# An mLSTM cell and a gated feed-forward block: the state's increments by products of 32 and of 8 weight columns instead of 40

## The chip, the cores and the metric

The kernel runs on one core of one Trainium2 chip. The metric is the device time in microseconds (us). The core has five engines that work side by side: TensorE (PE in the profile, its weight loads PEld) multiplies matrices, VectorE (DVE), ScalarE (ACT) and GpSimd (POOL) work element by element, and SyncE (SP) issues most of the transfers (DMAs). Matmul results land in PSUM, a memory of 128 partitions; all other tiles are in SBUF.

## The reference

Two blocks, one behind the other. The first is a recurrent cell over 768 steps, for 4 batches (B) and 8 heads (H) of 40 dimensions (D). Each head has a state `C` of 40 x 40 and a normalizer `n` of 40:

```python
for t in range(S):
    m_new = np.maximum(f_gate[:, :, t] + m, i_gate[:, :, t])
    f_stab = np.exp(f_gate[:, :, t] + m - m_new)
    i_stab = np.exp(i_gate[:, :, t] - m_new)
    C = f_stab * C + i_stab * outer(vt, kt)          # per batch and head
    n = f_stab * n + i_stab * kt
    y[:, :, t] = sigmoid(o_gate[:, :, t]) * (C @ qt) / max(abs(n @ qt), 1)
```

(shown with the subscripts of batch and head left out). The second block takes the 3072 x 320 rows that come out: `h = x @ w_in` (320 x 2048), `g = h * cos(h)`, `out = g @ w_out` (2048 x 320).

## The kernel before

**Cells.** The sequence is cut into six chunks of 128 steps. A cell is one chunk of one batch, all eight heads; cell n is chunk n // 4 of batch n % 4, so there are 24. Within a cell the recurrence is done as products over the 128 steps. The state of each batch (`st[b]`) is carried from chunk to chunk: after a cell it is faded and an increment is added, the sum over 128 steps of weighted keys times values. This increment is what the change is about. It is needed for all chunks but the last, so in cells 0 to 19.

**The increment.** `weigh_k` (line 408) makes the weighted keys `kw` on GpSimd, 128 steps x 8 heads x 64, of which 40 columns are used. `seam(n)` (line 586) multiplies on TensorE: for each of four pairs p of heads and each j of a pair, the 128 x 40 keys are the weights that are loaded and 48 value columns (`DV`: 40 of values and 8 of ones, for the normalizer) move past them. The 40 x 48 result lands in the PSUM tile `pu`, on partitions 64 j to 64 j + 40, in column block p. So two products, j = 0 and j = 1, stand side by side in `pu`, and four pairs behind each other. A product of float32 numbers is done in two passes, and has two weight loads (LDWEIGHTS) and two matmuls (MATMUL) in the profile: 20 cells x 8 products are 320 records of each.

**Who stands before and behind.** `seam` is called by `first_cells` for the cells 0 to 3, by `first_period` for cell 4 and by `both_parts` for the others. In cells 0 to 3 it first turns the cell's output with four products (`px`, lines 592 and 594; those of 594 load 64 weight columns) and then makes the increment; behind it come the products of the next cell (`ph`, line 491) or warming matmuls. From cell 4 on there is no `px`: the increment follows directly on `values(n)` (line 483), whose products `vt` (lines 501 to 510) load 32 weight columns, or 16, move 128, and land four side by side on partitions 32 a:

```python
nc.tensor.matmul(vt[32 * a:32 * a + 32, i], vs(n)[:, h, 0:32], E[:, h], start=True, stop=False)
```

Behind it come the products of the second block's next pair of hidden tiles (`pup`, lines 644 and 650).

**Who reads `pu`.** `state(n)` (line 619) adds it to `st[b]`, in four pieces: on ScalarE (line 625) for cells 0 to 3, on VectorE (line 627) for the others. It reads partitions 64 j to 64 j + 40, as before. The loads of k and v of later cells (`load_two`, line 330, on SyncE's queue) write into buffers that `weigh_k` and the increment's products have read.

**The second block** is woven between the cells, in chunks of 512 rows (four batches): class `Up` (line 632) makes pairs of hidden tiles `pup`, ScalarE and VectorE make `g` from them (`near`, `rest`, `sin`, `gate`, lines 657 to 672), and `down` (line 674) or `products` (line 731, tile `acc`) multiply by `w_out`. In the first 130 us or so the weights come in, as pairs of 32-bit words that lines 144 to 162 turn into float32.

**Order.** The order of the instructions on every engine is written out by hand (`first_cells`, `first_period`, `both_parts` under a manual schedule); each engine works through its own queue in that order, and semaphores are put in where a tile is handed over. SyncE's queue issues transfers in the order written.

Of the kernel before, what the change touches and what calls it, by code (L numbers as in the profile page):

```python
# [29 lines left out]
def kernel(  # L30
# [20 lines left out]
    nc = tc.nc  # L51

    B, H, S, D = q.shape
# [231 lines left out]
    sig, xT, xL, Es, kws, qkT, pss, heads_of, raw_o, Gs, early = {}, {}, {}, {}, {}, {}, {}, {}, {}, {}, {}  # L285
# [10 lines left out]
    def vs(n):  # L296
        return vs2[n // 2 % 2][:, n % 2]
# [121 lines left out]
    def psum(n):  # L419

        return (ps_o, "o") if n < B and n % 2 == 1 else (ps_a, "a")
# [164 lines left out]
    def seam(n):  # L586

        pool, tag = psum(n)
        if n < B:
            px = pool.tile([128, NK + 1, C], FP, name="px", tag=tag)  # L590
            for i in range(NK):
                nc.tensor.transpose(px[:, i], ys[n][:, ts(i, 128)], ident)
            for e in range(2):
                nc.tensor.matmul(px[64 * e:64 * e + 64, NK], ys[n][:, KL:DM], ident, start=True, stop=True)
            pxs[n] = px
        if n < N - B:
            pu = pool.tile([128, HP, DV], FP, name="pu", tag=tag)
            for p in range(HP):
                for j in range(2):
                    h = 2 * p + j  # L600
                    nc.tensor.matmul(pu[64 * j:64 * j + D, p], kws[n][:, h, 0:D], vs(n)[:, h], start=True, stop=True)  # L601
            pus[n] = pu

    def low_out(n):
# [229 lines left out]
    def first_cells():  # L834
# [53 lines left out]
        turn_out(2, False)  # L888
        warm(2)
        seam(0)  # L890
        weigh(1)
        seam_out(0)
# [10 lines left out]
        turn(3)  # L903
        sigmoid(0, slice(2, 4))
        seam(1)
        load_two(B, "Kv")
        outs.append((0, weights_out(0)))
# [10 lines left out]
        scores(3)  # L918
        warm(1)
        seam(2)  # L920
        weigh(3)
        take_apart(*pieces[0])
# [245 lines left out]
```

## Time and profile before

| | |
|---|---|
| time, median of 3 runs | 534.6 us (534.35 to 534.88) |
| profiled execution: its own time | 531.87 us |
| profiled execution: span from first to last instruction | 530.1 us |
| mean granted TensorE clock in it | 0.988 |
| TensorE's weight loads, busy | 346.9 us |
| VectorE busy | 406.9 us |
| ScalarE busy | 286.6 us |
| GpSimd busy | 247.9 us |
| moved by DMA | 57.81 MB |

The profile is of one execution, and its durations are of that one. A row of a group tells the line of the code, the engine, the operation, the tile written and those read, the shapes (128*40 128x48 is 128 rows by 40 weight columns, with 48 moving columns on 128 partitions) and how many there were. Matmuls overlap each other, and their ends are modelled; so differences of starts say more than durations, and the chain of waits, which goes back from the last instruction to what released each step, says which engine's time counts. "issue" stands for time in which an engine waited for nothing that the profile shows.

The group of the changed line, by the view of one line (duration in ns: least, median, most; first and last start):

```profile
L601 PEld LDWEIGHTS pu<-vs,kw x320: 112/117/184, 22.9 to 361.6; 128*40 128x40 f32 x160
L601 PE MATMUL pu<-vs,kw x320: 206/206/303, 23.0 to 361.7; 128*40 128x48 f32 x160
```

### The profile page before, as it was taken

To read this page: it belongs to the slowest core of one execution; us is meant where nothing else is said; L and a number is where in the kernel's file an instruction comes from. 1 tells how busy PE (TensorE), PEld (TensorE's weight loads), DVE (VectorE), ACT (ScalarE), POOL (GpSimd) and SP (SyncE) were. 2 spreads that over 40 slices of the span, in tenths; PEclk is the share of its full clock that TensorE was granted. 3 is DMA by queue.
4 is the path that set the end of the run, shared out by engine and by line. 5 is a ranking of instruction groups with operands and counts; after the bars stand their busy time and mean duration, and the time that the engine had idled before them with its cause. 6 is when DMAs were issued, how large, how long until landed. Compare 5 with 4: busy or idle time off the path is not lost.

```text
span 530.1 us, 10427 instructions
## 1 busy us (share of the span) xinstructions
PE 512.8 (97%) x3848; PEld 346.9 (65%) x3848; DVE 406.9 (77%) x828; ACT 286.6 (54%) x546; POOL 247.9 (47%) x409
## 2 busy tenths in 40 slices
PE   7999779999999999999999999999999999999996
PEld 3875354556657666676677677677667676666765
DVE  4896798997778878888778888868898878664636
ACT  2896797857556537744547635537735531312221
POOL 7536454673775684554454554453433333121211
PEclk9999879999999999999999999999999999999999
DMA  9999999999339259149159149159110000000001
GB/s 139 227 183 213 231 195 231 246 238 208 48 118 196 56 109 181 41 120 170 56 116 157 42 113 176 49 116 160 47 56 6 1 6 6 26 25 1 1 0 50
DMA packets 97762, 57.81 MB, mean 109 GB/s; under 512 B 62048, under 2 KB 89792, under 8 KB 97712
## 3 DMA queue, kind: packets, MB, share of 16 engines
q1 hardware_dynamic: 96240, 55.64, 51.1%
q0 software_dynamic: 1424, 1.49, 1.4%
q8 instruction: 30, 0.49, 0.4%
q14 instruction: 20, 0.16, 0.1%
q10 hardware_dynamic: 48, 0.02, 0.0%
HBM read 51.71 MB, written 4.11 MB: 105 GB/s over the span
## 4 chain that ended last, share of the span: by engine, by line
PE 81%; DVE 7%; DMA 6%; POOL 1%; issue 1%; SPq 1%; ACT 1%; DVEq 0%; POOLq 0%
PE pup L650 26%; PE acc L760 25%; PE pup L644 8%; PE ps L475 4%; PE po L682 3%; PE late L760 3%; DMA bits<-in_moe_w_in_dram 3%; PE vt L510 2%; PE vt L501 2%; PE pu L601 2%; DMA o<-in_o_gate_dram 1%; PE pw L832 1%; DVE t L456 1%; PE ph L491 1%; DMA bits<-in_moe_w_out_dram 1%
## 5 line engine op out<-in xcount | busy, mean ns | idle before, releaser
L650 PE MATMUL pup<-xT,w_in_sb 128*128 128x512 f32 x384 | 176.7, 603 | 3.1 <-DVE g L670 2.9
L658 ACT ACTIVATE n<-pup 128x512 int32<-128x512 f32 x96 | 54.0, 595 | 193.6 <-PE pup L644 141.6
L650 PEld LDWEIGHTS pup<-xT,w_in_sb 128*128 128x128 f32 x384 | 70.4, 191 | 90.3 <-issue 88.0
L661 DVE SCALAR_TENSOR_TENSOR n<-pup,n 128x512 f32<-128x512 f32 x96 | 63.0, 687 | 82.3 <-ACT n L658 80.9
L724 POOL TENSOR_TENSOR D<-g 128x128 f32<-128x128 f32 x40 | 19.7, 492 | 145.6 <-DVE g L670 145.6
L666 ACT ACTIVATE n<-n 128x512 f32<-128x512 f32 x96 | 59.3, 631 | 16.1 <-DVE n L661 16.1
L670 DVE SCALAR_TENSOR_TENSOR g<-pup,n 128x512 f32<-128x512 f32 x96 | 61.9, 684 | 2.2 <-ACT n L666 1.4
L760 PE MATMUL acc<-w_out_sb,g 128*128 128x160 f32 x320 | 58.6, 304 | 0.0
L760 PE MATMUL acc<-T,g 128*128 128x160 f32 x320 | 58.0, 301 | 0.1
L644 PE MATMUL pup<-xL,w_in_l 64*128 64x512 f32 x192 | 55.2, 650 | 0.9 <-POOL w_in_l L162 0.9
L607 POOL DMA_DIRECT2D xL<-xT x40 | 22.5, 563 | 65.1 <-DVE xT L538 61.6
L760 PEld LDWEIGHTS acc<-w_out_sb,g 128*128 128x128 f32 x320 | 47.8, 190 | 5.6 <-issue 4.2
L760 PEld LDWEIGHTS acc<-T,g 128*128 128x128 f32 x320 | 48.1, 190 | 3.7 <-issue 3.0
L406 ACT ACTIVATE E<-E,tab 128x128 f32<-128x128 f32 x160 | 49.0, 389 | 0.2
L682 PE MATMUL po<-w_out_sb,g 128*128 128x320 f32 x128 | 36.2, 436 | 0.0
L760 PE MATMUL acc<-T,S 128*128 128x160 f32 x160 | 35.0, 300 | 0.0
L475 PEld LDWEIGHTS ps<-t,t 40*128 40x128 f32 (+1 forms) x384 | 24.2, 187 | 12.6 <-DVE t L456 7.5
L682 PEld LDWEIGHTS po<-w_out_sb,g 128*128 128x128 f32 x128 | 24.0, 190 | 11.9 <-issue 1.9
L481 DVE TENSOR_TENSOR E<-ps,E 128x512 f32<-128x512 f32 x48 | 30.7, 680 | 1.4 <-PE ps L475 1.3
L644 PEld LDWEIGHTS pup<-xL,w_in_l 64*128 64x128 f32 x192 | 14.8, 187 | 24.0 <-issue 19.6
L760 PE MATMUL acc<-w_out_sb,S 128*128 128x160 f32 x160 | 28.8, 299 | 0.0
L962 ACT ACT_TABLE_LOAD x22 | 28.2, 1283 | 0.4
(178 smaller groups left out, 878.0 us busy)
## 6 DMA issues: line engine op xcount, KB each, us to landing
E<-M_d SPq DMA_DIRECT2D x22, 512.0 KB, 4.3
qr<-in_q_dram SPq DMA_DIRECT2D x36, 160.0 KB, 3.1
kr<-in_k_dram SPq DMA_DIRECT2D x36, 160.0 KB, 5.4
G<-G_d SPq DMA_DIRECT2D x20, 256.0 KB, 5.2
bits<-in_moe_w_out_dram SPq DMA_DIRECT2D x8, 640.0 KB, 5.8
bits<-in_moe_w_in_dram SPq DMA_DIRECT2D x16, 256.0 KB, 7.6
out_dram<-o_sb SPq DMA_DIRECT2D x24, 160.0 KB, 1.9
ks<-in_k_dram SPq DMA_DIRECT2D x10, 320.0 KB, 7.5
```

The lines of the kernel that those rows point to most:

```text
L406: nc.scalar.activation(out=Es[n][:, h], in_=Es[n][:, h], func=AF.Exp, scale=-1.0, bias=tab[:, c, 0, g:g + 1])
L475: nc.tensor.matmul(ps[j][:, p], kT[r, p], qT[r, p], start=True, stop=True)
L481: nc.vector.tensor_tensor(out=w, in0=pss[n][j], in1=w, op=OP.mult)
L644: nc.tensor.matmul(pu, w_in_l[r, f2], xL[c][r].rearrange("p b t -> p (b t)"), start=ahead, stop=not ahead)
L650: nc.tensor.matmul(pu.rearrange("p (b t) -> p b t", b=B), w_in_sb[:, i, ts(2 * f2 + e, 128)], xT[c][:, i:NK * B:NK], start=(i == 0 and not ...
L658: nc.scalar.activation(out=self.n[e], in_=self.pu[e], func=AF.Copy, bias=0.25)
L661: nc.vector.scalar_tensor_tensor(out=self.n[e].bitcast(FP), in0=self.pu[e], scalar=0.25, in1=self.n[e], op0=OP.add, op1=OP.subtract)
L666: nc.scalar.activation(out=r, in_=r, func=AF.Sin, scale=TWO_PI_DOWN)
L670: nc.vector.scalar_tensor_tensor(out=g, in0=self.pu[e], scalar=TWO_PI, in1=self.n[e].bitcast(FP), op0=OP.mult, op1=OP.mult)
L682: nc.tensor.matmul(po[c][b], gs[c, f][:, ts(b, C)], w_out_sb[:, f], start=(f == 0), stop=(f == NF - 1))
L760: nc.tensor.matmul(a, lhs, rhs, start=start, stop=stop)
L962: nc.scalar.activation(out=spot, in_=spot, func=AF.Sin)
```

## The change

In `seam`, each product of 40 weight columns is made as two: one of the columns 0 to 32, whose result goes to the partitions 64 j to 64 j + 32, and one of the columns 32 to 40, whose result goes to the partitions 64 j + 32 to 64 j + 40. Both move the same 48 value columns. The results lie where they lay before, and nothing else is changed.

```diff
             for p in range(HP):
                 for j in range(2):
                     h = 2 * p + j
-                    nc.tensor.matmul(pu[64 * j:64 * j + D, p], kws[n][:, h, 0:D], vs(n)[:, h], start=True, stop=True)
+                    for lo, hi in ((0, 32), (32, D)):
+                        nc.tensor.matmul(pu[64 * j + lo:64 * j + hi, p], kws[n][:, h, lo:hi], vs(n)[:, h], start=True, stop=True)
             pus[n] = pu
```

The line numbers behind line 600 are one higher in the changed kernel.

## The prediction

> **What bounds the kernel now.** First the page's busy line and its slices, then the chain of waits (what ended last, in order of time), then the timeline around one cell's increments, then the waits of TensorE and of the DMA queue.
>
> ```profile
> PE 512.8 (97%) x3848; PEld 346.9 (65%) x3848; DVE 406.9 (77%) x828; ACT 286.6 (54%) x546; POOL 247.9 (47%) x409
> ...
> DMA  9999999999339259149159149159110000000001
> ```
>
> TensorE is busy 97% of the span. The DMA slices are 13.25 us each (530.1 / 40): ten nines mean that the DMA engines are full for the first 132 us. In that stretch the chain of waits mixes engines (it holds weight transfers at 42.95, 82.57 and 108.77 us). From 116.34 us to 381 us it names TensorE alone; the waits of TensorE between 140 and 375 us have not one entry. So a nanosecond off TensorE in that stretch is a nanosecond off the end, and before it one has to ask.
>
> The changed products are the eight of line 601 in each cell, two matmul records each (320 in 20 cells). The chain of waits at cell 8, one piece to a row (start us, us, what):
>
> ```profile
> 144.04 0.22 PE vt L504 x8
> 144.26 0.22 PE vt L507 x8
> 144.48 0.22 PE vt L510 x8
> 144.70 0.47 PE pu L601 x16
> 145.17 1.06 PE pup L644 x4
> ```
>
> And the same products in cell 1, behind other neighbours:
>
> ```profile
> 27.54 0.22 PE px L592 x2
> 27.76 0.37 PE px L594 x4
> 28.13 0.34 PE pu L601 x16
> 28.47 1.91 PE ph L491 x16
> ```
>
> Sixteen records of one kind cost 0.47 us in cell 8 and 0.34 us in cell 1. What differs is what stands before them. Shapes tell it: vt's products load 32 or 16 weight columns, pu's 40, px L594's 64, px L592's 128. The built program marks the part of the array for each: 32 columns wide for vt, 64 for pu and for L594, 128 for L592. Behind the same width there is no surcharge (L504 to L507 to L510, though 16 columns follow 32; L594 to pu). Behind another width there is: pu after vt 0.47 against 0.34, px L594 0.37 for four records where vt takes 0.22 for eight of the same 128 moving columns.
>
> Where the surcharge sits, in the timeline of cell 7 (start us, us, engine, line, shapes, count, idle before):
>
> ```profile
> 123.05 0.40 PE L507 MATMUL vt<-E,vr 128*16 128x128 f32 x8
> ...
> 123.27 0.40 PE L510 MATMUL vt<-qG,st 128*32 128x128 f32 x8
> 123.60 0.41 PEld L601 LDWEIGHTS pu<-vs,kw 128*40 128x40 f32 x16 [0.20 <-issue]
> 123.60 0.54 PE L601 MATMUL pu<-vs,kw 128*40 128x48 f32 x16
> ```
>
> vt's groups begin 0.22 us apart; pu begins 0.33 us after the last. Its first weight load could not be brought forward under vt's products, as every load inside vt is.
>
> **The change part by part.** Each product of 40 weight columns becomes one of 32 and one of 8, on neighbouring parts of the array, marked 32 wide. Nothing moves in any queue, no wait is added and no DMA touched; the order of all other instructions on the five engines is the same. TensorE gets 160 more products, 320 more matmul records and as many weight loads.
>
> (1) *Entry from vt, cells 4 to 19.* vt and pu are now of one width, so the surcharge of 0.47 - 0.34 = 0.13 us goes. Bounds: 0 if the gap had another cause, 0.13 if it goes whole. I take 0.13, by the three same-width borders above.
>
> (2) *The products themselves.* Now two parts of the array work side by side, so 16 records are 8 passes: 0.34 / 8 = 42.5 ns a pass of 48 moving columns. After, four parts side by side, 32 records, again 8 passes. No row shows four parts with 48 columns. From below: 42.5 ns, the present pass, since the same 48 columns go through. From above: the four go two by two, 85 ns. vt is nearest, it has four parts of 32 columns: 8 records are two passes in 0.22 us, 0.11 us for 128 columns, 0.86 ns a column, or 41 ns for 48. So 42.5 ns, and the products cost what they cost. That four can start fast enough is seen in a slice of the timeline 30 ns wide:
>
> ```profile
> 142.96 0.32 PE L501 MATMUL vt<-E,vs 128*32 128x128 f32 x4
> ```
>
> Four records of some 0.30 us each (mean 286 ns) fit into 0.32 us: their starts lie within about 20 ns, 7 ns apart. Four starts of 7 ns are 28 ns, less than a pass; the two added parts put the last start 0.014 us later, which I leave in the rounding.
>
> (3) *Weight loads.* 32 + 8 + 32 + 8 = 80 columns a pass, as 40 + 40 = 80 now; no more to load in the same time, only in more pieces.
>
> (4) *Exit to L644 (or ph L491).* A change of width before, and one after: 0.
>
> (5) *Entry from px L594, cells 0 to 3.* These were of one width with pu and no longer are: the 0.13 us appears there. For cells 0, 1 and 2 pu is on the chain (at 23.18, 28.13, 32.81 us); in cell 3 the chain has left through px to ScalarE. So +0.4 us at most. What can cover it is the DMA: the chain runs into transfers at 42.95 us (6.57 us), 49.54 (7.59) and 57.15 (4.69), at times when all 16 DMA engines are full, so that a request made later only waits less. From 0 to +0.4; I take half, +0.2.
>
> (6) *Cells 4, 5 and 6, before the 116 us mark.* 0.13 us less each on TensorE, of which cells 5 (78.53 us, 0.82 us at a low clock) and 6 (101.94 us) lie on the chain. The queue of loads hangs on these products:
>
> ```profile
> SPq L345 <- PE pup L650: 20.8, 8, 3.4
> ...
> SPq L345 <- PE pu L601: 4.6, 1, 4.6
> ```
>
> (waits of the DMA queue: total us, times, longest). An earlier end lets the load of k and v go earlier, into full DMA engines. From 0 to -0.4; I take -0.2, and (5) and (6) cancel.
>
> (7) *Cells 7 to 19*, from 123.4 us on, 13 cells on the pure TensorE chain: 13 x 0.13 = 1.7 us. Is there room for it on the other engines? In the densest stretch read (220 to 240 us) VectorE is busy 18.05 of 20 us; a cell of about 20 us gets 0.13 us shorter, and 1.95 us are free. Behind pu stands L644, which needs the buffers that gate L670 frees; in cell 8 that gate ended at 142.03 us, 3 us ahead of L644.
>
> Sum: -1.7 + 0.2 - 0.2 = -1.7 us, bounds of (5) and (6) included -2.1 to -1.3. The profiled execution took 531.87 us (span 530.1 and 1.8 around it): 530.2 after. The median of the runs is 534.6, 2.7 above that execution, so I carry the difference over: **532.9 us**.
>
> One rule speaks against (2). The Trainium skill, page "TensorE: Matmul & The Clock Gate", section "Wait — 56ns, not 53.3ns?", says that matmuls start no closer than about 25 ns however few columns they move. By that, 32 records would be an estimated 0.80 us, 0.33 more than now, and 13 cells would cost 4.3 us: 538.9. The trace does not bear it out across parts of the array: pu's 16 records in 0.34 us are 21 ns apart on average, and vt's four start 7 ns apart.
>
> **The rivals.**
>
> *A floor per record (slower).* If the 21 ns per record of today (0.34 / 16) are what issuing a load and a matmul takes, and not the 48 columns, then 32 records take 0.68 us. That is +0.21 us in cells 4 to 19, and +0.34 with the new surcharge of 0.13, so +0.47, in cells 0 to 2. 13 x 0.21 = +2.7; the early cells add 0 to 3 x 0.47 + 3 x 0.21 = 2.0. Middle +3.7: 538.3 us. It decides from 0.47 / 32 = 15 ns a record on. For it: no row sustains more than one record in 21 ns. Against it: the 7 ns starts, and that 42.5 ns a pass is just what 48 columns take at vt's 0.86 ns a column, so that the columns explain the whole pass.
>
> *The gap before pu is a wait, not a width.* The waits of line 601 put 12 of its 16 gaps down to vt L507 and 4 to nothing. If pu really waited for vt's products, the late start (0.33 - 0.22 = 0.11 us) would stay and only the slower first pass be saved, some 0.02: 13 x 0.02 = 0.3 us, 534.3. Against: the gaps are some 0.2 us whichever name they carry, and px L594 has one (0.17) behind L592 with no wait at all.
>
> *The gain is swallowed.* Either the first cells cost their whole 0.4 and the middle ones give nothing, or another engine takes the time back at the borders between chunks, where VectorE is on the chain (381 to 394 us). 1.7 - 0.4 = 1.3, less about half: -0.6, 534.0. For it: 14 us of VectorE on the chain there. Against: that stretch begins with vt L510 on TensorE, so it moves forward with it.
>
> *The change does not do what it says.* Other marks of the array than assumed: the built program has 32-wide ones for all 16 products, so I give it nothing.
>
> **How the numbers follow.** Forecast 0.68 (532.9, own range 532.3 to 533.4: the bounds of (5) and (6), and 0.1 to 0.2 for the medians, whose three runs lie within 0.5). Wait or swallowed together 0.21 (534.0 to 534.6). Floor 0.09 (537.3 to 539.3), 0.02 for anything else slower. This measurement can tell about 0.2%, 1.07 us, from no change: below 533.53 is faster, 0.69 with the edge of the swallowed case; within, 0.20; slower, 0.11. The range 532.1 to 534.7 holds all but the floor and the odd cases.
>
> **What would show it.** Right: in the chain, pu from cell 4 on at about 0.34 us with 32 records, vt's last group to pu 0.22 us, no idle time before its weight load; in cells 0 to 2 about 0.47. TensorE's start-to-start from vt's last group to L644 falls from 0.80 us (123.27 to 124.07) to about 0.67. L644's own 1.06 is unchanged. Wrong: pu near 0.68 (floor), pu still 0.11 us late (a wait), or pu at 0.34 with the span of 116 to 376 us unshortened (swallowed).

## The result, and the profile after

The changed kernel took 531.35 us (median of 10 runs, 530.14 to 532.59) against 534.01 us for the kernel before in the same measurement (10 runs, 532.83 to 534.88). The ratio is 0.9951, with a 95% interval of 0.9937 to 0.9964: 2.7 us faster, between 1.9 and 3.4. The forecast was 1.7 us faster and 532.9 us, in a range of 532.1 to 534.7; the time lies below that range. Three more measurements of the same kernel, told below, give a smaller gain: 2.1 us over all four.

The profiled execution of the changed kernel has a span of 530.2 us (531.94 us in all), that of before 530.1 us. The two single executions are as long as each other, because the stretch before cell 7 happened to take 117.7 us in the one and 116.3 in the other; the change shows in them all the same. The chain of waits at cell 8, one piece to a row (start us, us, what); line 602 is the old line 601, 645 the old 644, 651 the old 650, 671 the old 670:

```profile
145.15 0.22 PE vt L504 x8
145.36 0.22 PE vt L507 x8
145.58 0.22 PE vt L510 x8
145.80 0.34 PE pu L602 x32
146.14 1.06 PE pup L645 x4
```

Twice as many records, and 0.34 us instead of 0.47. The timeline of the same place has pu 0.22 us behind vt's last group, as one vt group stands behind another:

```profile
145.18 0.40 PE L507 MATMUL vt<-E,vr 128*16 128x128 f32 x8
145.40 0.40 PE L510 MATMUL vt<-qG,st 128*32 128x128 f32 x8
145.62 0.52 PE L602 MATMUL pu<-vs,kw 128*32 128x48 f32 x32
146.07 1.13 PE L645 MATMUL pup<-xL,w_in_l 64*128 64x512 f32 x4
```

From vt's last group to L645 it is 0.67 us, where it was 0.80. The view of line 602 has no wait for vt L507 any more; four gaps are left, those of cells 0 to 3:

```profile
L602 PE MATMUL pu<-vs,kw x640: 206/206/230, 22.0 to 361.8; 128*32 128x48 f32 x132, 128*8 128x48 f32 x28
...
  issue: 0.7, 4
```

There the gap that was foreseen has come. In the timeline of weight loads at cell 1, L594 loads 64 columns, and pu's first load starts only after a gap of 0.17 us; in the trace of before there is no gap at this place:

```profile
26.67 0.20 PEld L594 LDWEIGHTS px<-ident,y 128*64 128x64 f32 x4 [0.17 <-DVE E L481]
27.04 0.41 PEld L602 LDWEIGHTS pu<-vs,kw 128*32 128x32 f32 x32 [0.17 <-issue]
```

**Where the saving went.** The start of each TensorE product in the trace of after, less the start of the same product in the trace of before, steps down by 0.130 or 0.131 us at each of the 13 increments from cell 7 to cell 19, 1.70 us together. But it steps up again in five places: at 153.08 us of the old trace (0.13), 176.79 (0.10), about 195 (0.07), 234.71 (0.10) and 314.77 (0.10), 0.50 together. The chain of after at the first of them:

```profile
150.83 3.26 PE acc L761 x24
154.09 0.10 issue
154.19 3.67 PE pup L651 x8
157.86 1.06 PE pup L645 x4
158.92 1.02 PE ps L475 x16
```

`pup` products of this kind, between `acc` and L645, take 3.43 us elsewhere in this chain (at 173.35 us), and `ps` 0.89. What they wait for is in VectorE's timeline:

```profile
151.25 1.29 DVE L662 SCALAR_TENSOR_TENSOR n<-pup,n 128x512 f32<-128x512 f32 x2 [2.15 <-ACT n L659]
152.46 0.86 DVE L628 TENSOR_TENSOR st<-st,pu 40x128 f32<-40x128 f32 x4
153.35 1.29 DVE L671 SCALAR_TENSOR_TENSOR g<-pup,n 128x512 f32<-128x512 f32 x2
```

The first of the two gates of L671 ends at about 154.0 us and frees the buffer into which `pup` is written from 154.19 on. The four additions of the state (L628, 0.86 us) stand ahead of it. At the other four places it is the turning of k (L456), which ends just as `ps` begins:

```profile
176.55 1.07 DVE L456 STREAM_TRANSPOSE t<-kr 128x512 f32<-128x512 f32 x1
...
177.67 0.97 PEld L475 LDWEIGHTS ps<-t,t 40*128 40x128 f32 x16 [0.66 <-DVE t L456]
```

So of 1.70 us on TensorE 1.20 reach the end. That was to be seen before the change, in two views. The old chain has

```profile
153.12 3.64 PE pup L650 x8
...
157.81 0.99 PE ps L475 x16
```

where rows of the same kind are 3.43 (at 172.35 us) and 0.89 (at 176.84): at 153.12 VectorE is late already. At the four turnings the rows of the old chain are 0.89 or 0.94, and there it is the weight loads that show how close VectorE is. In the old trace the first load of `ps` stands like this at one of the four places (176.55) and at one that lost nothing (254.18):

```profile
176.55 0.99 PEld L475 LDWEIGHTS ps<-t,t 40*128 40x128 f32 x16 [0.54 <-DVE t L456]
...
254.18 0.19 PEld L475 LDWEIGHTS ps<-t,t 40*128 40x128 f32 x2 [0.24 <-issue]
```

At the four places the turning of k ended 0.11 to 0.18 us before `ps` began, and 0.6 to 1.4 us before it elsewhere from cell 8 on, but for cell 9, whose `ps` (the row at 157.81) was waiting already. The waits of TensorE's matmuls name none of this, because in the profile the matmul ahead is still running while the load waits; those of its weight loads between 140 and 375 us do (us in total, times, longest):

```profile
PEld ps L475 <- DVE t L456: 3.1, 6, 0.7
```

### The profile page after: what moved, and what is told of

It reads as the page before. It is cut to its first block, busy times and chain, and to the rows that moved or that the text cites. A ratio compares the mean times of both kernels' runs of the same rounds, so it can differ in the third digit from the quotient of the medians.

```text
span 530.2 us, 11067 instructions
## 1 busy us (share of the span) xinstructions
PE 510.7 (96%) x4168; PEld 347.7 (66%) x4168; DVE 405.3 (76%) x828; ACT 286.6 (54%) x546; POOL 247.8 (47%) x409
## 4 chain that ended last, share of the span: by engine, by line
PE 78%; DMA 8%; DVE 4%; ACT 3%; SPq 3%; POOL 2%; issue 1%; DVEq 0%; ACTq 0%; POOLq 0%
PE pup L651 27%; PE acc L761 25%; PE pup L645 8%; PE po L683 4%; PE ps L475 3%; PE late L761 3%; PE vt L510 2%; PE vt L501 2%; DMA bits<-in_moe_w_out_dram 2%; DMA E<-M_d 2%; DMA low<-in_moe_w_in_dram 1%; DMA G<-G_d 1%; DMA bits<-in_moe_w_in_dram 1%; PE pu L602 1%; SPq L328 1%
## 5 line engine op out<-in xcount | busy, mean ns | idle before, releaser
L671 DVE SCALAR_TENSOR_TENSOR g<-pup,n 128x512 f32<-128x512 f32 x96 | 61.9, 684 | 2.3 <-ACT n L667 1.5
L645 PE MATMUL pup<-xL,w_in_l 64*128 64x512 f32 x192 | 54.2, 641 | 1.4 <-POOL w_in_l L162 1.3
L683 PE MATMUL po<-w_out_sb,g 128*128 128x320 f32 x128 | 37.4, 446 | 0.1
L645 PEld LDWEIGHTS pup<-xL,w_in_l 64*128 64x128 f32 x192 | 14.4, 184 | 24.9 <-issue 20.2
```

Of the source, the lines that this page charges most:

```text
L645: nc.tensor.matmul(pu, w_in_l[r, f2], xL[c][r].rearrange("p b t -> p (b t)"), start=ahead, stop=not ahead)
L671: nc.vector.scalar_tensor_tensor(out=g, in0=self.pu[e], scalar=TWO_PI, in1=self.n[e].bitcast(FP), op0=OP.mult, op1=OP.mult)
L683: nc.tensor.matmul(po[c][b], gs[c, f][:, ts(b, C)], w_out_sb[:, f], start=(f == 0), stop=(f == NF - 1))
```

## The experiments

All but the first row are timed in five rounds, beside the kernel before on the same chip. The "late stretch" is the time in one trace from cell 7's first score product to the last instruction. Over seven traces with the old products in it (before and the kernels below) it is 413.66 to 413.85 us, so it repeats to 0.2 us; what comes before it, with the DMA engines full, takes 116.3 to 120.1 us.

| kernel | median us (runs) | before us (runs) | ratio (95%) | late stretch us |
|---|---|---|---|---|
| changed, first measurement | 531.35 (10) | 534.01 (10) | 0.9951 (0.9937 to 0.9964) | 412.48 |
| only_first | 533.46 (12) | 533.66 (35) | 1.0005 (0.9982 to 1.0028) | 413.85 |
| only_mid | 533.28 (12) | 533.66 (35) | 0.9991 (0.9974 to 1.0007) | 413.80 |
| only_late | 532.13 (12) | 533.66 (35) | 0.9965 (0.9946 to 0.9984) | 412.58 |
| all_again | 531.59 (12) | 533.66 (35) | 0.9961 (0.9945 to 0.9978) | 412.57 |
| moving_halves | 536.54 (12) | 533.90 (29) | 1.0049 (1.0033 to 1.0065) | 417.05 |
| only_rest | 531.54 (12) | 533.90 (29) | 0.9962 (0.9945 to 0.9980) | 412.46 |
| vector_ahead | 530.40 (6) | 533.90 (29) | 0.9932 (0.9910 to 0.9954) | 411.71 |
| vector_ahead_old_width | 532.53 (12) | 533.90 (29) | 0.9976 (0.9957 to 0.9995) | 412.97 |
| mid_thrice | 533.19 (12) | 533.39 (24) | 0.9991 (0.9978 to 1.0004) | 413.68 |
| first_thrice | 534.31 (12) | 533.39 (24) | 1.0017 (0.9998 to 1.0036) | 413.79 |
| vector_ahead_narrow | 529.77 (6) | 533.39 (24) | 0.9928 (0.9908 to 0.9948) | 411.16 |
| all_third | 531.36 (8) | 533.39 (24) | 0.9949 (0.9929 to 0.9969) | 412.58 |
| unchanged | 534.29 (12) | 533.43 (35) | 1.0012 (0.9995 to 1.0029) | 413.66 |
| all_fourth | 531.73 (12) | 533.43 (35) | 0.9964 (0.9946 to 0.9983) | 412.44 |
| only_late_again | 531.34 (12) | 533.43 (35) | 0.9966 (0.9949 to 0.9984) | 412.44 |
| only_mid_again | 533.02 (12) | 533.43 (35) | 0.9989 (0.9975 to 1.0002) | 413.78 |

### The change by its cells

Three kernels split the increment in some cells alone, one is the changed kernel again.

```diff
-                    for lo, hi in ((0, 32), (32, D)):
+                    for lo, hi in ((0, 32), (32, D)) if n < B else ((0, D),):             # only_first
+                    for lo, hi in ((0, 32), (32, D)) if B <= n < B + 3 else ((0, D),):    # only_mid
+                    for lo, hi in ((0, 32), (32, D)) if n >= B + 3 else ((0, D),):        # only_late
```

only_first:

> Only cells 0 to 3 are split; their increments follow px of another width, and the entry costs 0.13 us each in the trace in every theory. Theory P (as predicted: three entries on the chain, half hidden by the DMA): +0.2 us, between 0 and +0.4. Theory F (the unexplained 1.5 us of the early stage come from these cells, whose later end shifts what the transfers collide with): -1.0 to -1.5 us. Theory S (any more TensorE records shift the early stage, wherever they stand): about -0.5 us.

only_mid:

> Only cells 4, 5 and 6 are split; each saves 0.13 us on TensorE. Theory P: -0.2 us, between 0 and -0.4. Theory M (the earlier end lets the loads of k and v go earlier, and the early stage gains by more than the time saved on TensorE): -1.0 to -1.5 us. Theory F: 0 to -0.4.

only_late:

> Only cells 7 to 19 are split. By the trace of the change 8 of the 13 savings of 0.13 us come through and 5 turn into new waits for VectorE: -1.1 us (theories F and M). If all of the measured difference comes from here, -2.6 us; if the new waits are an accident of that execution, -1.7 us.

all_again:

> The changed kernel once more on the same chip, as the yardstick: -2.6 us (interval of the first measurement -1.9 to -3.4). If the parts add up, only_first + only_mid + only_late give the same. If it comes out near -1.1 to -1.7, the early stage had given nothing and the first measurement lay high.

The late cells alone give -1.9 us by the ratio (-2.9 to -0.9), and -1.2 in the late stretch (413.75 to 412.58); the five steps back stand in this trace at the same places and of the same size, so they are no accident. The first cells give 0.3 us (-1.0 to +1.5), the middle ones -0.5 (-1.4 to +0.4): the intervals hold the forecast's +0.2 and -0.2, and shut out that either is worth 1.5, though not that the middle ones are worth 1. The parts add to -2.1, which is all_again's own -2.1. So the first measurement gave 0.5 us more than its repeat.

### More records without the narrower width

moving_halves keeps 40 weight columns and moves the 48 value columns in two halves.

```diff
-                    nc.tensor.matmul(pu[64 * j:64 * j + D, p], kws[n][:, h, 0:D], vs(n)[:, h], start=True, stop=True)
+                    for lo, hi in ((0, DV // 2), (DV // 2, DV)):
+                        nc.tensor.matmul(pu[64 * j:64 * j + D, p, lo:hi], kws[n][:, h, 0:D], vs(n)[:, h, lo:hi], start=True, stop=True)
```

> Twice the matmul records at the old width: all 40 weight columns, the 48 value columns moved as 24 and 24. Width theory: the entry of 0.13 us stays, a pass of 24 columns takes 20 to 23 ns, so 32 records take 0.34 to 0.40 us behind the same 0.13: 0 to +0.06 us a cell, 0 to +1.0 us in all. Floor theory (21 ns for each record): 0.68 us and the entry, +0.34 us a cell, +4 to +7 us. If more records alone made the kernel faster, as the change did: -1 us or better.

It is 2.6 us slower, and neither number fits. The timeline at cell 8:

```profile
145.97 0.40 PE L510 MATMUL vt<-qG,st 128*32 128x128 f32 x8
146.31 0.82 PE L602 MATMUL pu<-vs,kw 128*40 128x24 f32 x32
147.06 1.13 PE L645 MATMUL pup<-xL,w_in_l 64*128 64x512 f32 x4
```

The entry is there as in the old kernel (0.34 us after vt's group), since the width is the old one. But the 32 records start over 0.62 us: 16 passes of 38 to 39 ns each, hardly less than the 42.5 ns of 48 columns. The width theory had 20 to 23. What stayed the same is what is loaded, 40 columns, and the likeliest reading is that a pass on one part of the array is no shorter than the loading of its weights; ph of line 491, which loads 128 columns and moves 41, agrees with 1.91 us for 16 records, 119 ns each. A floor of 38 ns for one part of the array, whatever it loads, was not told apart from this. It is no price of a record over the whole array: in the changed kernel 32 records start over 0.32 us, 10 ns each, because four parts of the array share them. So more TensorE records at the old width make the kernel slower, not faster.

### Cells 4 to 19, and VectorE out of the way

only_rest splits in cells 4 to 19 (`n >= B`). vector_ahead takes the five waits away: in the second half of each period, from the second chunk on, the gates come before the state's additions, and q and k are turned before the sums.

```diff
-                if cell:
+                if cell and c == 0:
                     state(n)
                 for e in range(2):
                     up.sin(e)
                     up.gate(e)
+                if cell and c > 0:
+                    state(n)
+                    if n + 1 < N:
+                        turn_blocks(n + 1)
                 if c > 0:
                     sums(c, f2)
...
                 if cell and n + 1 < N:
-                    turn_blocks(n + 1)
+                    if c == 0:
+                        turn_blocks(n + 1)
                     scale_q(n + 1)
```

only_rest:

> Cells 4 to 19 split, cells 0 to 3 as before. The stretch from cell 7's scores to the end loses 1.2 us as in the changed kernel (413.8 to 412.5 us). Theory P (the early entries cost, half hidden): 0.2 us faster than the changed kernel, about -2.4 us against before. Theory F (the first cells' split helps the early stage): only -1.2 to -1.7 us.

vector_ahead:

> The changed kernel, and from the second chunk on VectorE makes the gates before it adds the state's increments, and turns q and k before it makes the sums. If the five savings of 0.13 us were lost in waits for VectorE, these waits go and the stretch from cell 7's scores to the end falls from 412.5 to 412.1 us or below: 0.5 us or more faster than the changed kernel, about -2.6 to -3.5 us against before. If the five waits have another cause, the stretch stays at 412.5 us.

vector_ahead_old_width:

> The same order on VectorE with the old products of 40 columns. The trace of before shows some 0.5 us of waits for VectorE in the stretch from cell 7's scores on (413.8 us). If only those go: 413.3 to 413.8 us, 0 to -0.5 us against before, and the split is then worth its full 13 x 0.13 = 1.7 us between this kernel and vector_ahead. If the new order is worth as much with either width, the split is worth 1.2 us between the two.

only_rest gives -2.0 us by the ratio, with all_again's -2.1; the first four cells' split is neither a help nor a loss that can be seen. vector_ahead is at 530.40 us, its ratio 0.9932. Its chain at the place of the first wait:

```profile
151.54 3.26 PE acc L761 x24
154.80 3.43 PE pup L651 x8
158.23 1.06 PE pup L645 x4
159.29 0.89 PE ps L475 x16
```

3.43 and 0.89: the waits are gone, and with them every step back between cells 8 and 19. The late stretch of this trace is 411.71 us; the execution lost 0.45 us at 137 us, where vector_ahead_narrow, told below, has the same code, loses nothing and comes to 411.16. With the old width the new order gives 412.97 us. Product by product, the starts of vector_ahead_narrow less those of vector_ahead_old_width step down by 0.130 or 0.131 us at each of the 13 increments and nowhere up: the split's 1.70 us come through whole when VectorE is out of the way. This shows the five waits to be the cause of what was missing.

The order by itself is worth 0.8 us of 413.75 with the old width, more than the 0 to 0.5 that were expected. Against the trace of before, 0.3 us of it come where VectorE was late already (from 153 to 196 us), and 0.4 at 394 us: the chain of before runs over VectorE from 381 to 394 us, and that of vector_ahead_old_width stays on TensorE there.

### The early cells, with larger levers

mid_thrice and first_thrice issue each product three times with the same result, on the old width, in cells 4 to 6 or in cells 0 to 3. The expectations take 0.68 us more for a cell; in the traces it is 0.80 (the row of pu in the chain is 1.27 us instead of 0.47 in cell 6, and 1.14 instead of 0.34 in cells 0 to 2), so 2.4 us more in cells 4 to 6, and as much in cells 0 to 2. vector_ahead_narrow is vector_ahead with `px` of 32 columns in cells 0 to 3.

```diff
+                    for _ in range(3 if B <= n < B + 3 else 1):       # mid_thrice; first_thrice: n < B
                         nc.tensor.matmul(pu[64 * j:64 * j + D, p], kws[n][:, h, 0:D], vs(n)[:, h], start=True, stop=True)
...
-                nc.tensor.matmul(px[64 * e:64 * e + 64, NK], ys[n][:, KL:DM], ident, start=True, stop=True)
+                for lo in (0, 32):                                    # vector_ahead_narrow
+                    nc.tensor.matmul(px[64 * e + lo:64 * e + lo + 32, NK], ys[n][:, KL + lo:KL + lo + 32], ident, start=True, stop=True)
```

mid_thrice:

> The old width, but in cells 4, 5 and 6 each product of the increment is issued three times with the same result: 3 x 0.68 = 2.0 us more on TensorE there. It measures how much of TensorE's time in these cells reaches the end. As predicted (a half, between nothing and all): +1.0 us, 0 to +2.0. If these cells' saving of 0.39 us was worth the unexplained 1 us of the change, the slope is over 2 and this costs +4 us or more.

first_thrice:

> The same in cells 0 to 3: 3 x 0.68 = 2.0 us more on TensorE ahead of the chain's exit from cell 2, and 0.68 us in cell 3. As predicted (a half): +1.0 us, 0 to +2.0. If the transfers hide these cells wholly: 0. If a later start here helps the early stage: -1 us or better.

vector_ahead_narrow:

> vector_ahead, and in cells 0 to 3 the two products of px with 64 weight columns become four of 32, so that px and the increment are of one width. TensorE loses the 0.13 us entry in each of these cells. If the first cells reach the end by half: 0.2 us faster than vector_ahead; if the transfers hide them: the same time, about 530.4 us (-3.4 us against before).

all_third:

> The changed kernel a third time, as the yardstick of this chip: -1.2 us from the late cells, as in every trace so far, and what the early cells give: -0.4 us if they give just what is saved on TensorE there (-1.6 in all), -0.9 to -1.4 us more if they give what the first two measurements had left over (-2.1 to -2.6 in all).

2.4 us more in cells 4 to 6 cost nothing: -0.5 us (-1.2 to +0.2). Something else hides these cells' TensorE work, and what is saved there cannot have come through by being shorter. It is likely the transfers, since the chain of mid_thrice's trace goes through them almost without a break from 43 to 78 us; no run changed the transfers. In cells 0 to 2 the same 2.4 us cost 0.9 (-0.1 to +1.9), some four tenths, where the forecast took a half. all_third, the changed kernel beside them, is 2.7 us faster by its ratio (1.7 to 3.8), 2.0 by the medians. In vector_ahead_narrow the entry goes where it was predicted to go; the timeline of cell 1 has pu 0.25 us behind the `px` group, and no gap:

```profile
26.27 0.38 PE L592 MATMUL px<-ident,y 128*128 128x128 f32 x2
26.58 0.42 PE L595 MATMUL px<-ident,y 128*32 128x128 f32 x8
26.83 0.52 PE L603 MATMUL pu<-vs,kw 128*32 128x48 f32 x32
27.28 1.98 PE L491 MATMUL ph<-vs,E 128*128 128x41 f32 x16
```

At 529.77 us (6 runs), 3.6 us below before, it is the fastest version run here; by how much it beats vector_ahead cannot be told from the two intervals.

### What is left over, and whether the comparison is fair

> The kernel before, unchanged, measured as the others are. If the comparison is fair: 0, within 0.4 us. If it favours whatever is measured against before: -0.3 to -0.6 us, and all other results are to be read that much slower.

> The changed kernel: -2.3 us by the mean of the three measurements. Against unchanged rather than against before: -1.2 us if the early stage gives nothing, -1.6 if it gives what TensorE saves in cells 4 to 6, -2 or more if the early stage truly gains 1 us.

> Cells 7 to 19 alone: -1.2 us by the trace, -1.5 in the first measurement. Against all_fourth it is slower by what cells 0 to 6 give: 0 to 0.4 us as predicted, 1 us if the early stage is the cause.

> Cells 4 to 6 alone: 0 if the transfers hide them, as mid_thrice says; -0.4 as in the first measurement, or if their 0.39 us came through whole; -1 us if they are the cause of the open 1 us.

The kernel before, measured as if it were changed, came out 0.9 us slower than itself in the same measurement (12 runs beside 35; ratio 1.0012, 0.9995 to 1.0029). So the comparison does not favour what is measured against before, and it is no finer than this: twelve runs can lie 0.9 us off. all_fourth gave -1.7 us by the medians, only_late_again -2.1, only_mid_again -0.4. Weighted by their scatter, the means of the four measurements of the change give -2.1 us (plus or minus 0.3), the two of the late cells -1.8 (0.45), the two of the middle cells -0.55 (0.37).

## Why the prediction was wrong in its number

**The entry and the products, steps (1) to (4): right, to a hundredth.** 0.47 became 0.34, pu 0.22 us behind vt, four parts side by side with no floor per record. The rival of a floor fell by the change itself (10 ns a record, where it needed 15), the rival of a wait by the gaps that are gone. The Trainium skill, page "TensorEngine Tiling (Array Packing)", section "Tiling Modes", says that a change of tiling mode drains TensorE. The trace agrees as far as it goes: 0.13 us are lost at vt's border, are gone when the width is the same, and are there again at px's.

**The 25 ns floor** of the Trainium skill (page "TensorE: Matmul & The Clock Gate", section "Wait — 56ns, not 53.3ns?") does not hold across parts of the array: 32 records in 0.32 us are 10 ns each. Within one part the shortest passes of the runs here are 38 ns (moving_halves).

**Step (7), the size: 1.7 us, measured 1.2.** "The waits of TensorE between 140 and 375 us have not one entry", and so all 13 savings were let through. That view holds the matmuls' waits; the one of the weight loads has six entries for VectorE's turning. Five savings met a VectorE that was already late or just in time, by the first order of its queue: four additions ahead of a gate, the sums ahead of a turning. Only one gate, 3 us early, had been looked at; and VectorE's busy share, 18.05 of 20 us, says nothing about the one instruction that is late. vector_ahead shows it. The rival of a swallowed gain had this much right, that VectorE takes time back; but it named the border at 381 to 394 us, which the gain passes whole. This error by itself makes the time longer than forecast; that it came out shorter has the two reasons that follow, the level and an early stage that is not explained.

**Steps (5) and (6).** For the first cells "I take half, +0.2": first_thrice's 0.9 of 2.4 us is near that half, though its interval also takes in none, and only_first's 0.3 cannot be told from nothing. For cells 4 to 6 the -0.2 was wrong in its reason: by the interval of mid_thrice at most 0.2 of 2.4 us of TensorE's time there reach the end.

**The level.** "The median of the runs is 534.6, 2.7 above that execution, so I carry the difference over", with 0.1 to 0.2 us "for the medians, whose three runs lie within 0.5". This step did most to put the time out of the range: from 534.01 the same range would have begun at 531.5, and the time would have lain 0.16 below it instead of 0.75. The same kernel has a median of 533.6 us over all 145 runs of it, single runs from 531.3 to 536.6; three runs close together were no measure of that. Of the 1.55 us between 532.9 and 531.35, 0.6 is the level (534.6 against 534.01), 1.0 the change (2.66 against 1.7), and of this 0.5 did not come back in the repeats.

**What stays open.** The traces give 1.2 us in the late stretch, all runs together 2.1 (1.8 to 2.5). By that, some 0.6 to 1.3 us lie in the early stage, which a single trace cannot show since it varies by 3.7 us from one execution to the next. Less TensorE time in cells 4 to 6 is not the reason (mid_thrice was no slower), and the entries in cells 0 to 3 should have cost. The split of the early cells is perhaps not needed for it at all: only_late has it nowhere before cell 7, and its two measurements together give 1.8 us (1.3 to 2.2), where its traces give 1.2. The granted clock explains little: its mean is 0.993 over the 42 runs of the changed kernel and 0.991 over the 135 runs of before for which it is on record, and within either set 0.001 less of it goes with 0.10 to 0.14 us more, which makes an estimated 0.2 us. The unchanged kernel's 0.9 us says how far such a remainder may be trusted. No run here settles it.

## What to carry to other kernels

Put products of the same array width behind each other: a border between widths costs 0.13 us here, and cutting a product in two cost nothing here, where the pieces lie on different parts of the array and together load as many columns as before (moving_halves, whose pieces share a part, was 2.6 us slower). Before counting a saving once for each round of a loop, compare the rows of the chain that should be alike: one that is 0.1 us longer than its sisters is a wait already, even when the waits of the matmuls do not name it. And read the waits of the weight loads beside them, which name an engine that is only just in time. And a median of three runs that agree is not a level; where transfers set the pace, forecast the difference and let the range hold the level's own scatter.

## What the hardware showed that was not expected

- A pass of 24 moving columns behind 40 loaded ones takes 38 to 39 ns, one of 48 takes 42.5: moving half as much bought next to nothing.
- The price of a border differs with what stands before it, in the two cases here: by the starts of single records, from the last one to the next product it is 0.20 us behind 128 moving columns (vt to the old pu) and 0.135 us behind 48 (pu to L645), where the same width needs 0.09 behind vt.
- 2.4 us of added TensorE work, in a stage in which TensorE is on the chain of waits in the profile (cells 5 and 6 of before), cost nothing. A place on the chain of one execution is not yet a price.
